# Loading the first third of the weights from SyncE's queue at the start of a fused FFT and ReGLU kernel

## The chip, the cores and the metric

The kernel runs on one core of a Trainium2 chip. The metric is the device time of one execution in microseconds (us). A ratio is the mean time of one kernel's fast runs over the mean of the other's from the same rounds, with a 95% interval, so it is not quite the ratio of the medians that are quoted beside it.

## The reference

```
x: 8 x 3008 x 256;  w_gate, w_val: 256 x 1536;  w_out: 1536 x 256   (float32)
X = real(fft(fft(x, axis=1), axis=2))            # Fourier mixing over sequence and model axis
x = X.reshape(24064, 256)
out = (maximum(x @ w_gate, 0) * (x @ w_val)) @ w_out
```

## The kernel before

The transform over the sequence is split as 94 x 32 ("stage 1" and "stage 2"); the transform over the model axis is folded into the weights: W's upper and lower 128 rows are added and subtracted, and a cosine or sine matrix (cd) is multiplied onto them ("fold"). The weights are prepared in thirds of 512 columns. The first batch has no predecessor to hide behind: its x comes in six pieces ("lo" for rows 0 to 15, "hi" for rows 16 to 31), cast from float32 to bf16 by the DMA.

```python
def load_w(n, q, which=(0, 1)):                 # one third of W_gate and W_val: four pieces of 256 KB
    for i in which:
        w = (w_gate, w_val)[i]
        for c in range(2):
            q.dma_start(out=wst[i, n, c], in_=w[c*128:(c+1)*128, n*512:(n+1)*512])
def pair_w(n, i, eng, parts=(0, 1)):            # sum into a third tile, difference in place
    lo, hi, up = (wst[i, n, c] for c in range(3))
    if 0 in parts: eng.tensor_tensor(up, lo, hi, op=ALU.add)
    if 1 in parts: eng.tensor_tensor(lo, lo, hi, op=ALU.subtract)
def fold_w(n, i, cs, ps=None):                  # TensorE, then ScalarE writes wc or ws
    for k, w in ((0, wst[i, n, 2]), (1, wst[i, n, 0])):
        nc.tensor.matmul(ps[64*k:64*k+64, :], lhsT=cd[:, cs, 64*k:64*k+64], rhs=w, start=True, stop=True)
    nc.scalar.copy((wc, ws)[cs][i][:, n*512:(n+1)*512], ps[:])
# ... cut ...
warm(WARM)                                      # 12 dummy matmuls at the start
iota(pl, si...); iota(pl, ki...)                # GpSimd (pl), in order
load_first(0, 8); ...; load_first(24, 8)        # x pieces, on GpSimd's queue
load_first(8, 4); load_first(20, 4); ...; load_first(12, 4); load_first(16, 4)
# ... cut ...
load_w(0, pl)                                   # W's first third, behind x on the same queue
# ... stage 1 tables; ends() and back() make reversed copies of each x piece on VectorE and ScalarE ...
group((1, 2, 3), False); warm(9)                # stage 1: lo products of banks 1 to 3, dummies
# ... VectorE: da, dq (for cd), bit tables ... then the hi pieces
group((1, 2, 3), True)
group((4, 5), False); warm(4); group((4, 5), True); group((6, 7, 0), False)
pair_w(0, 0, dve); group((6, 7, 0), True)       # W_gate's sum and difference on VectorE
# ... cut ...
pair_w(0, 1, pl)                                # W_val's on GpSimd
fold_w(0, 0, 0, g_tile()); upright(...); upright(...)
fold_w(0, 0, 1, psw); rotate(...); scale_w(0, 0, psw); stage2(...)
fold_w(0, 1, 0, g_tile()); stage2(...); fold_w(0, 1, 1)
# ... then 288 steps of G (gate), V (value), h and out ...
```

Of the kernel before, what the change touches and what calls it, by code (L numbers as in the profile page):

```python
# [11 lines left out]
F32 = mybir.dt.float32  # L12
BF16 = mybir.dt.bfloat16
I32 = mybir.dt.int32
ALU = mybir.AluOpType
# [13 lines left out]
def free(ap, offset, *dims):  # L29

    part = list(ap.ap[0])
    return bass.AP(ap.tensor, ap.offset + offset, [part] + [list(d) for d in dims])
# [12 lines left out]
def kernel(ctx: ExitStack, tc, x, w_gate, w_val, w_out, out):  # L45
# [3 lines left out]
    nc = tc.nc  # L49
# [14 lines left out]
    psg = ctx.enter_context(tc.tile_pool(name="psg", bufs=2, space=PS))  # L64
# [90 lines left out]
    t1t = {}  # L155
# [27 lines left out]
    psf = {}  # L183
# [41 lines left out]
    def first_evac(c, evac):  # L225

        if 0 not in t1t:
            t1t[0] = tp.tile([128, 16, D], BF16, tag="t1", bufs=1, name="t1")
        dst = free(t1t[0][:], 2 * c, [1536, 2], [16, 96], [1, 2])
        src = free(psf[c], 0, [96, 2], [1, 96], [192, 2])  # L230
        plain = nc.scalar.copy if evac == "act" else nc.vector.tensor_copy
        plain(dst, src)
        if c == 0:
            plain(free(t1t[0][0:1], 1536, [16, 96]), psf[0][0:1, 384:480])

    def upright(blk, cs, evac):

        if 0 not in t4t:
            t4t[0] = tp.tile([128, NKA, D], BF16, tag="t4", name="t4")
        ps = spare("pst") if blk else early("pst")  # L240
        for g in range(4):
            nc.tensor.matmul(ps[:, g * H:(g + 1) * H], lhsT=free(t1t[0][:], 1536 * cs + 128 * (4 * blk + g), [1, 128]),  # L242
                             rhs=perm[:], start=True, stop=True)
        dst, src = t4t[0][:, 4 * blk:4 * blk + 4, cs * H:(cs + 1) * H], ps.rearrange("p (g d) -> p g d", g=4)
        if evac == "act":
            nc.scalar.copy(dst, src)
        else:
            nc.vector.tensor_copy(dst, src)
# [17 lines left out]
    def stage2(b, blk, cs, evac):  # L266
        if (b, blk) not in pqt:
            pqt[b, blk] = pqp.tile([128, 2, 512], BF16, tag="pq", name="pq")
            nbt[b, blk] = pqp.tile([128, 512], BF16, tag="nb", name="nb")
        t4, pq = t4t[b], pqt[b, blk]  # L270
        ps = borrow("ps2") if b else early("ps2") if blk == 0 else spare("ps2")
        for g in range(4):
            nc.tensor.matmul(ps[:, g * 128:(g + 1) * 128], lhsT=t4[:, 4 * blk + g, cs * H:(cs + 1) * H],  # L273
                             rhs=m2[:, cs, :], start=True, stop=True)
        if blk == NBLK - 1:
            nc.tensor.matmul(ps[:, 496:497], lhsT=t4[:, 0, cs * H:(cs + 1) * H], rhs=m2[:, cs, 0:1], start=True, stop=True)
        if evac == "act":
            nc.scalar.copy(pq[:, cs, :], ps[:])
        else:
            nc.vector.tensor_copy(pq[:, cs, :], ps[:])  # L280
        if cs == 1 and (b or blk):

            row = view(Nd, (b * NBLK + blk) * 512, [[512, 1], [1, 512]])
            nc.sync.dma_start(out=row, in_=pq[0:1, 1, :])
            nc.sync.dma_start(out=nbt[b, blk][:], in_=view(row, 0, [[0, 128], [1, 512]]))
# [5 lines left out]
    m2 = const.tile([128, 2, 128], BF16, tag="m2")  # L291
    rot = const.tile([128, 128], BF16, tag="rot")
    perm = const.tile([128, 128], BF16, tag="perm")
    s2 = const.tile([128, 1], F32, tag="s2")
    wc = [const.tile([128, DF], BF16, tag=f"wc{i}", name=f"wc{i}") for i in range(2)]
    ws = [const.tile([128, DF], BF16, tag=f"ws{i}", name=f"ws{i}") for i in range(2)]
    wm = [const.tile([128, DF], BF16, tag=f"wm{i}", name=f"wm{i}") for i in range(2)]
# [7 lines left out]
    wst = {}  # L305
# [4 lines left out]
                wst[i, n, c] = pair[:, i, :]  # L310
    cd = hp.tile([128, 2, 512], F32, tag="h", name="cd")[:, :, 0:H]

    def load_w(n, q, which=(0, 1)):
        for i in which:
            w = (w_gate, w_val)[i]
            for c in range(2):
                q.dma_start(out=wst[i, n, c], in_=w[c * 128:(c + 1) * 128, n * 512:(n + 1) * 512])

    def pair_w(n, i, eng, parts=(0, 1)):

        lo, hi, up = (wst[i, n, c] for c in range(3))
        if 0 in parts:
            eng.tensor_tensor(up, lo, hi, op=ALU.add)
        if 1 in parts:
            eng.tensor_tensor(lo, lo, hi, op=ALU.subtract)

    def scale_w(n, i, ps):

        nc.vector.tensor_scalar(wm[i][:, n * 512:(n + 1) * 512], ps[:], scalar1=s2[:], scalar2=None, op0=ALU.mult)

    def fold_w(n, i, cs, ps=None):

        ps = ps or spare("psw")
        for k, w in ((0, wst[i, n, 2]), (1, wst[i, n, 0])):
            nc.tensor.matmul(ps[64 * k:64 * k + 64, :], lhsT=cd[:, cs, 64 * k:64 * k + 64], rhs=w,  # L335
                             start=True, stop=True)
        sl_ = slice(n * 512, (n + 1) * 512)
        nc.scalar.copy((wc, ws)[cs][i][:, sl_], ps[:])
        if cs and (n or i):
            scale_w(n, i, ps)  # L340
# [8 lines left out]

    with tc.tile_pool(name="sp", bufs=1, space=SB) as sp:  # L350
        dve, pl = nc.vector, nc.gpsimd

        def residue(t, q, n, eng):

# [14 lines left out]
        def iota(eng, out, pattern, base, mult):  # L369
            eng.iota(out, pattern=pattern, base=base, channel_multiplier=mult, allow_small_or_imprecise_dtypes=True)  # L370
# [8 lines left out]
        mi = sp.tile([128, 1], F32, tag="mi")  # L379
        dd = sp.tile([128, H], F32, tag="dd")  # L380
# [4 lines left out]
        ui = sp.tile([128, 4, NB], F32, tag="ui")  # L385
        di = sp.tile([128, 4, 2, 16], F32, tag="di")
# [9 lines left out]
        def warm(n):  # L396

            for k in range(n):
                nc.tensor.matmul(psk[:], lhsT=wk[:, 512:640], rhs=wk[:, 0:512], start=True, stop=True)
# [14 lines left out]
        iota(pl, free(dd[:], 0, [64, 2], [1, 64]), [[1, 2], [2, 64]], 0, 0)  # L414
        load_first(12, 4)
        load_first(16, 4)
        pl.tensor_scalar(perm[:], dd[:], scalar1=mi[:], scalar2=None, op0=ALU.is_equal)
        iota(pl, ui[:], [[1, 4], [0, NB]], 0, 0)
        iota(pl, kbi[:, 0, :], [[1, NB]], NB // 2, 0)
        iota(pl, kbi[:, 1:4, :], [[0, 3], [1, NB]], 0, 0)  # L420
        load_w(0, pl)

        def angles(lo, hi):
            t, q = tt[:, lo:hi, :], tq[:, lo:hi, :]
# [10 lines left out]
        def bits(shift, mask):  # L435
            ti = sp.tile([128, 1], I32, tag=f"b{shift}{mask}i")
            dve.tensor_scalar(ti[:], pi[:], scalar1=shift, scalar2=mask,
                              op0=ALU.logical_shift_right, op1=ALU.bitwise_and)
            tf = sp.tile([128, 1], F32, tag=f"b{shift}{mask}f")
            dve.tensor_copy(tf[:], ti[:])  # L440
            return tf
# [29 lines left out]
        absolute(dq[:], da[:])  # L471
        cosines(cd[:, 0, 1:H], dq[:, 1:H], D)
        sines(cd[:, 1, 1:H], da[:, 1:H], D, 1.0)
        jj, sl, up, odd = bits(0, 15), bits(4, 1), bits(5, 3), bits(0, 1)

        ends(24, 8)
        back(25, 3, "act")
# [15 lines left out]
        sv, ti = [], []  # L493
# [3 lines left out]
            sv.append(sp.tile([128, 4, NB], F32, tag=f"m2s{cs}", name="sv"))  # L497
            pl.tensor_scalar(ti[cs], kbi[:], scalar1=mul[:], scalar2=(o0, o1)[cs][:], op0=ALU.mult, op1=ALU.add)
        dve.tensor_scalar(tabs["wzn"][:], wz[:, 0], scalar1=-1.0, scalar2=None, op0=ALU.mult)
        dve.tensor_copy(cd[:, 1, 0:1], odd[:])  # L500
        dve.tensor_scalar(cd[:, 0, 0:1], odd[:], scalar1=-1.0, scalar2=1.0, op0=ALU.mult, op1=ALU.add)
        dve.tensor_scalar(ui[:], ui[:], scalar1=up[:], scalar2=-1.0, op0=ALU.is_equal, op1=ALU.mult)

        group((4, 5), False)
        warm(4)
        ends(20, 4)
        back(20, 4, "dve")
        group((4, 5), True)
# [9 lines left out]
        load_w(2, nc.sync)  # L518
        load_x(1, 0, nc.sync, False)
        first_evac(5, "act")  # L520
        pair_w(0, 0, dve)
        for cs in range(2):
            nc.scalar.activation(sv[cs][:], ti[cs], ACTF.Sin, scale=2.0 * math.pi / NB * (1.0 - 2e-7), bias=npi[:])
        group((6, 7, 0), True)
# [1 line left out]
        first_evac(7, "act")  # L526
        first_evac(0, "dve")
        for cs in range(2):
            dve.tensor_tensor(m2[:, cs, :].rearrange("p (u k) -> p u k", u=4), sv[cs][:], ui[:], op=ALU.mult)

        iota(pl, di[:], [[-32, 4], [-16, 2], [-1, 16]], 0, 1)
        pl.tensor_scalar(s2[:], mi[:], scalar1=1.0, scalar2=-2.0, op0=ALU.min, op1=ALU.mult)
        ro = rot[:].rearrange("p (u s j) -> p u s j", u=4, s=2)
        pl.tensor_scalar(ro[:, :, 0, 1:16], di[:, :, 0, 1:16], scalar1=16.0, scalar2=-1.0,
                         op0=ALU.is_equal, op1=ALU.mult)
        pl.tensor_scalar(ro[:, :, 1, 1:16], di[:, :, 1, 1:16], scalar1=-16.0, scalar2=None, op0=ALU.is_equal)
        pl.tensor_scalar(ro[:, :, :, 0], di[:, :, :, 0], scalar1=0.0, scalar2=None, op0=ALU.is_equal)

        def g_tile():
            return psg.tile([128, 512], F32, tag="g", name="psw")  # L540

        pair_w(0, 1, pl)
        pl.iota(ix[:], pattern=[[-1, 2], [4 * NA, B]], base=4 * NA - 1, channel_multiplier=-4)
        pl.tensor_scalar(ix[:], ix[:], scalar1=0, scalar2=None, op0=ALU.max)
        fold_w(0, 0, 0, g_tile())
        upright(0, 0, "act")
        upright(0, 1, "dve")
        psw = g_tile()
        fold_w(0, 0, 1, psw)
        rotate(0, 0, 4, dve.tensor_copy)  # L550
        scale_w(0, 0, psw)
        stage2(0, 0, 0, "act")
        fold_w(0, 1, 0, g_tile())
        stage2(0, 0, 1, "dve")
        fold_w(0, 1, 1)

        pair_w(1, 0, pl)
# [227 lines left out]
    n = len(steps) // 2  # L785
# [86 lines left out]
```

## Time and profile before

| | before |
|---|---|
| median, lowest, highest of three executions | 625.28, 624.44, 625.51 us |
| span of the profiled execution | 623.1 us |
| TensorE busy | 612.1 us, 98% |
| first x piece landed, "hi" piece landed | 6.1 us, 9.2 us |
| first hi product of stage 1, end of stage 1, first G matmul | 9.75, 15.62, 21.63 us |

The profile is read in this order. The page gives busy shares. The chain of work that ended last goes backwards from the last instruction and gives at each step what released it, so it says what the time consists of; a piece is one line with its start and length. The timeline then says, for one engine, what stood ahead of a piece and what it waited for (in square brackets). The lines that carry this are shown in the prediction.

### The profile page before, as it was taken

What the parts mean: (1) busy time and instruction counts of PE and PEld (TensorE: products, weight loads), DVE (VectorE), ACT (ScalarE), POOL (GpSimd) and SP (SyncE); (2) the same over time, 40 slices, a digit from 0 to 9 for tenths busy, and PEclk for the clock granted to TensorE, in tenths of its full rate; (3) what the DMA queues carried; (4) which work ended last, traced back from release to release, by engine and by line L of the source; (5) the groups of instructions that cost most, each with busy time, mean ns of one, the idle gap of its engine ahead of it and who ended that gap; (6) DMA issues with size and microseconds to landing.
All of it is one profiled execution on the core that took longest, in us unless ns stands there. A gap on an engine that the chain in (4) does not pass through costs nothing.

```text
span 623.1 us, 11916 instructions
## 1 busy us (share of the span) xinstructions
PE 612.1 (98%) x4252; PEld 409.3 (66%) x4284; DVE 536.5 (86%) x652; ACT 444.4 (71%) x855; POOL 520.2 (83%) x447
## 2 busy tenths in 40 slices
PE   8999999999999999999999999999999999999996
PEld 5345666666666666666667666766666666666665
DVE  7677898899889898988988998898988889899991
ACT  7677777777777767767777777767677676766660
POOL 8998998998898898899988998888988965555664
PEclk9999999999999999999999999999999999999998
DMA  8984282425452182613843255531822134112114
GB/s 169 241 163 114 83 220 77 123 66 169 118 145 71 41 228 79 155 36 89 221 102 90 66 162 126 138 77 34 223 82 59 34 86 124 52 34 67 34 35 99
DMA packets 42037, 67.44 MB, mean 108 GB/s; under 512 B 5877, under 2 KB 31774, under 8 KB 39962
## 3 DMA queue, kind: packets, MB, share of 16 engines
q1 hardware_dynamic: 37162, 50.61, 31.2%
q0 software_dynamic: 4656, 15.88, 10.8%
q8 instruction: 33, 0.54, 0.4%
q14 instruction: 26, 0.21, 0.1%
q10 hardware_dynamic: 160, 0.20, 0.1%
HBM read 38.85 MB, written 30.17 MB: 111 GB/s over the span
## 4 chain that ended last, share of the span: by engine, by line
PE 96%; DMA 1%; issue 1%; ACT 1%; DVE 1%; POOL 0%; POOLq 0%
PE po L685 40%; PE V L635 19%; PE G L619 10%; PE G L626 10%; PE G L620 10%; PE psw L335 2%; PE ps L164 2%; PE ps L273 2%; DMA hi<-in_x_dram,ixf 1%; PE ps L218 1%; PE pst L242 0%; PE ps L168 0%; ACT gs L621 0%; ACT gm L628 0%; DVE h L656 0%
## 5 line engine op out<-in xcount | busy, mean ns | idle before, releaser
L656 POOL TENSOR_TENSOR h<-gm,E 128x992 bf16<-128x992 f32 (+1 forms) x138 | 320.0, 2319 | 82.8 <-DVE E L663 52.0
L685 PE MATMUL po<-wo,h 128*128 128x256 bf16 (+2 forms) x2304 | 328.4, 272 | 0.4
L685 PEld LDWEIGHTS <-h 128*128 128x128 bf16 (+2 forms) x2304 | 231.4, 103 | 105.9
L628 ACT ACTIVATE gm<-G 128x496 f32<-128x496 f32 (+1 forms) x288 | 170.6, 592 | 94.2 <-PE G L626 87.2
L649 DVE TENSOR_TENSOR h<-gs,V 128x1024 bf16<-128x1024 f32 (+3 forms) x150 | 173.9, 1159 | 66.0 <-PE V L635 41.2
L642 DVE SCALAR_TENSOR_TENSOR E<-nb,af,V 128x496 f32<-128x496 bf16 (+1 forms) x276 | 190.2, 730 | 0.7 <-PE V L635 0.7
L621 ACT ACTIVATE gs<-G 128x497 f32<-128x497 f32 (+2 forms) x288 | 169.6, 589 | 23.7 <-PE G L620 23.7
L663 DVE SCALAR_TENSOR_TENSOR E<-E,V 128x992 f32<-128x992 f32 (+1 forms) x138 | 164.4, 1191 | 0.0
L619 PE MATMUL G<-pq,wc 128*128 128x496 bf16 (+2 forms) x286 | 107.2, 375 | 1.1
L626 PE MATMUL G<-pq,wm 128*128 128x496 bf16 (+1 forms) x288 | 107.9, 375 | 0.3
L620 PE MATMUL G<-pq,ws 128*128 128x497 bf16 (+2 forms) x288 | 107.9, 375 | 0.1
L635 PE MATMUL V<-pq,ws 128*128 128x496 bf16 (+2 forms) x280 | 83.7, 374 | 0.0
L635 PE MATMUL V<-pq,wc 128*128 128x496 bf16 (+2 forms) x267 | 80.9, 374 | 0.8 <-DVE h L656 0.8
L620 PEld LDWEIGHTS <-ws 128*128 128x128 bf16 x288 | 28.2, 98 | 32.6
L698 ACT COPY os<-po 128x512 f32<-128x512 f32 x63 | 36.9, 586 | 14.3 <-PE po L685 12.5
L115 POOL TENSOR_TENSOR eo<-xla 94x256 bf16<-94x256 f32 x56 | 40.7, 733 | 0.6
L635 PEld LDWEIGHTS <-wc 128*128 128x128 bf16 x288 | 28.2, 98 | 19.7 <-issue 1.3
L619 PEld LDWEIGHTS <-wc 128*128 128x128 bf16 x288 | 28.2, 98 | 19.1 <-issue 1.1
L179 ACT CAST t<-ps 96x512 bf16<-96x512 f32 x56 | 32.7, 584 | 4.0 <-PE ps L164 1.9
L115 POOL TENSOR_TENSOR eo<-xlb 94x256 bf16<-94x256 f32 (+1 forms) x42 | 34.5, 823 | 0.7
L112 POOL TENSOR_TENSOR xla<-xla,xha 94x510 f32<-94x510 f32 x28 | 32.9, 1175 | 2.2
L626 PEld LDWEIGHTS <-wm 128*128 128x128 bf16 x288 | 28.1, 98 | 4.4 <-issue 1.6
(140 smaller groups left out, 366.7 us busy)
## 6 DMA issues: line engine op xcount, KB each, us to landing
out_dram<-os SPq DMA_DIRECT2D x124, 128.0 KB
Td<-t SPq DMA_DIRECT2D x7, 768.0 KB
t<-Td SPq DMA_DIRECT2D x7, 768.0 KB
out_dram<-os SPq DMA_DIRECT2D x82, 64.0 KB
xla<-in_x_dram SPq DMA_DIRECT2D x7, 720.0 KB
xlb<-in_x_dram SPq DMA_DIRECT2D x6, 640.0 KB
nb<-Nd SPq DMA_DIRECT2D x23, 128.0 KB
out_dram<-os SPq DMA_DIRECT2D x40, 48.0 KB
```

Of the source, the lines that this page charges most:

```text
L115: yield eng.tensor_tensor(e1[:, :, k:k + H], x1[:, :, 0:H], free(x1, D, [DX, n], [-1, H]), op=op)
L619: nc.tensor.matmul(G[:, ds], lhsT=wc[0][:, fs], rhs=pq[:, 0, ds], start=True, stop=False)
L620: nc.tensor.matmul(G[:, ds], lhsT=ws[0][:, fs], rhs=pq[:, 1, ds], start=False, stop=True)
L621: nc.scalar.activation(pair(t, "gs")[:, t % 2, ds], G[:, ds], ACTF.Relu)
L626: nc.tensor.matmul(G[:, cols], lhsT=wm[0][:, f * 128:(f + 1) * 128], rhs=pqt[b, blk][:, 1, cols], start=False, stop=True, skip_group_check ...
L628: nc.scalar.activation(pair(t, "gm")[:, t % 2, cols], G[:, cols], ACTF.Relu)
L635: nc.tensor.matmul(o, lhsT=w[:, f * 128:(f + 1) * 128], rhs=pqt[b, blk][:, min(k, 1), cs], start=(k == 0), stop=(k > 0 or split(t)), skip_ ...
L642: nc.vector.scalar_tensor_tensor(pair(t, "E")[:, t % 2, cols], nbt[b, blk][:, cols], af[:, f:f + 1], pair(t, "V")[:, t % 2, cols], op0=ALU ...
L649: nc.vector.tensor_tensor(pair(t, "h")[:, k, 0, 0:ds.stop - ds.start], pair(t, "gs")[:, k, ds], val, op=ALU.mult)
L656: eng.tensor_tensor(free(pair(t, "h")[:], 1024 * (t % 2) + 512 + w - 1, [1024, n], [-1, w]), pair(t, "gm")[:, k, cols], val[:, :, cols], o ...
L663: nc.vector.scalar_tensor_tensor(E[:, :, cols], E[:, :, cols], 2.0, V[:, :, cols], op0=ALU.mult, op1=ALU.subtract)
L685: nc.tensor.matmul(po[0:m, i, :], lhsT=pair(t - f + ff, "h")[:, ff % 2, sg, g * 128:g * 128 + m], rhs=wo[:, ff, :], start=(ff == 0), stop= ...
```

## The change

Its intent is to take one of the four folds of the first third out of the stretch between stage 1 and the first G, and into a gap of stage 1 that dummy matmuls filled. For that W_gate has to be there early: three of the four W pieces become SyncE's first instructions, GpSimd sums W_gate, VectorE sums W_val later.

```diff
+        load_w(0, nc.sync, ((0, 0), (0, 1), (1, 0)))        # ahead of everything
 ...
-        pl.tensor_scalar(perm[:], dd[:], ...)
+        load_w(0, pl, ((1, 1),))
+        pair_w(0, 0, pl)
 ...
-        load_w(0, pl)
 ...
         group((4, 5), False)
-        warm(4)
+        fold_w(0, 0, 0, g_tile())
         ends(20, 4)
 ...
-        pair_w(0, 0, dve)
+        pair_w(0, 1, dve)
 ...
-            dve.tensor_tensor(m2[:, cs, :]..., sv[cs][:], ui[:], op=ALU.mult)
+            pl.tensor_tensor(m2[:, cs, :]..., sv[cs][:], ui[:], op=ALU.mult)
 ...
-        pair_w(0, 1, pl)
-        fold_w(0, 0, 0, g_tile())
+        psw = g_tile()
+        turned(0, 1, psw)                                   # the matmuls of a fold, without its copy
         upright(0, 0, "act")
         upright(0, 1, "dve")
+        nc.scalar.copy(ws[0][:, 0:512], psw[:])
+        nc.scalar.mul(wm[0][:, 0:512], psw[:], s2[:])
 ... (cut: the one-row piece of bank 0 goes to ScalarE, sign tables to GpSimd, two columns of cd earlier,
     ScalarE's copy of the third fold later)
```

More of the change, by code (lines that the diff above doesn't have):

```diff
@@ L233, in first_evac @@
         if c == 0:
-            plain(free(t1t[0][0:1], 1536, [16, 96]), psf[0][0:1, 384:480])
+            nc.scalar.copy(free(t1t[0][0:1], 1536, [16, 96]), psf[0][0:1, 384:480])
     def upright(blk, cs, evac):
@@ L311, with load_w @@
     cd = hp.tile([128, 2, 512], F32, tag="h", name="cd")[:, :, 0:H]
-    def load_w(n, q, which=(0, 1)):
-        for i in which:
+    def load_w(n, q, parts=((0, 0), (0, 1), (1, 0), (1, 1))):
+        for i, c in parts:
             w = (w_gate, w_val)[i]
-            for c in range(2):
-                q.dma_start(out=wst[i, n, c], in_=w[c * 128:(c + 1) * 128, n * 512:(n + 1) * 512])
+            q.dma_start(out=wst[i, n, c], in_=w[c * 128:(c + 1) * 128, n * 512:(n + 1) * 512])
     def pair_w(n, i, eng, parts=(0, 1)):
@@ L329, in scale_w, with turned @@
         nc.vector.tensor_scalar(wm[i][:, n * 512:(n + 1) * 512], ps[:], scalar1=s2[:], scalar2=None, op0=ALU.mult)
-    def fold_w(n, i, cs, ps=None):
-        ps = ps or spare("psw")
+    def turned(n, cs, ps, i=0):
         for k, w in ((0, wst[i, n, 2]), (1, wst[i, n, 0])):
@@ L336, in fold_w @@
                              start=True, stop=True)
+    def fold_w(n, i, cs, ps=None):
+        ps = ps or spare("psw")
+        turned(n, cs, ps, i)
         sl_ = slice(n * 512, (n + 1) * 512)
@@ L416 @@
         load_first(16, 4)
-        pl.tensor_scalar(perm[:], dd[:], scalar1=mi[:], scalar2=None, op0=ALU.is_equal)
+        load_w(0, pl, ((1, 1),))
+        pair_w(0, 0, pl)
         iota(pl, ui[:], [[1, 4], [0, NB]], 0, 0)
@@ L473 @@
         sines(cd[:, 1, 1:H], da[:, 1:H], D, 1.0)
-        jj, sl, up, odd = bits(0, 15), bits(4, 1), bits(5, 3), bits(0, 1)
+        odd, jj, sl, up = bits(0, 1), bits(0, 15), bits(4, 1), bits(5, 3)
+        dve.tensor_copy(cd[:, 1, 0:1], odd[:])
+        dve.tensor_scalar(cd[:, 0, 0:1], odd[:], scalar1=-1.0, scalar2=1.0, op0=ALU.mult, op1=ALU.add)
         ends(24, 8)
@@ L499, with g_tile @@
         dve.tensor_scalar(tabs["wzn"][:], wz[:, 0], scalar1=-1.0, scalar2=None, op0=ALU.mult)
-        dve.tensor_copy(cd[:, 1, 0:1], odd[:])
-        dve.tensor_scalar(cd[:, 0, 0:1], odd[:], scalar1=-1.0, scalar2=1.0, op0=ALU.mult, op1=ALU.add)
-        dve.tensor_scalar(ui[:], ui[:], scalar1=up[:], scalar2=-1.0, op0=ALU.is_equal, op1=ALU.mult)
+        pl.tensor_scalar(ui[:], ui[:], scalar1=up[:], scalar2=-1.0, op0=ALU.is_equal, op1=ALU.mult)
+        pl.tensor_scalar(perm[:], dd[:], scalar1=mi[:], scalar2=None, op0=ALU.is_equal)
+        iota(pl, di[:], [[-32, 4], [-16, 2], [-1, 16]], 0, 1)
+        pl.tensor_scalar(s2[:], mi[:], scalar1=1.0, scalar2=-2.0, op0=ALU.min, op1=ALU.mult)
+        def g_tile():
+            return psg.tile([128, 512], F32, tag="g", name="psw")
         group((4, 5), False)
-        warm(4)
+        fold_w(0, 0, 0, g_tile())
         ends(20, 4)
@@ L528 @@
         for cs in range(2):
-            dve.tensor_tensor(m2[:, cs, :].rearrange("p (u k) -> p u k", u=4), sv[cs][:], ui[:], op=ALU.mult)
-        iota(pl, di[:], [[-32, 4], [-16, 2], [-1, 16]], 0, 1)
-        pl.tensor_scalar(s2[:], mi[:], scalar1=1.0, scalar2=-2.0, op0=ALU.min, op1=ALU.mult)
+            pl.tensor_tensor(m2[:, cs, :].rearrange("p (u k) -> p u k", u=4), sv[cs][:], ui[:], op=ALU.mult)
         ro = rot[:].rearrange("p (u s j) -> p u s j", u=4, s=2)
@@ L537 @@
         pl.tensor_scalar(ro[:, :, :, 0], di[:, :, :, 0], scalar1=0.0, scalar2=None, op0=ALU.is_equal)
-        def g_tile():
-            return psg.tile([128, 512], F32, tag="g", name="psw")
-        pair_w(0, 1, pl)
         pl.iota(ix[:], pattern=[[-1, 2], [4 * NA, B]], base=4 * NA - 1, channel_multiplier=-4)
         pl.tensor_scalar(ix[:], ix[:], scalar1=0, scalar2=None, op0=ALU.max)
-        fold_w(0, 0, 0, g_tile())
+        psw = g_tile()
+        turned(0, 1, psw)
         upright(0, 0, "act")
         upright(0, 1, "dve")
+        nc.scalar.copy(ws[0][:, 0:512], psw[:])
+        nc.scalar.mul(wm[0][:, 0:512], psw[:], s2[:])
         psw = g_tile()
-        fold_w(0, 0, 1, psw)
+        turned(0, 0, psw, 1)
         rotate(0, 0, 4, dve.tensor_copy)
-        scale_w(0, 0, psw)
         stage2(0, 0, 0, "act")
-        fold_w(0, 1, 0, g_tile())
         stage2(0, 0, 1, "dve")
+        nc.scalar.copy(wc[1][:, 0:512], psw[:])
         fold_w(0, 1, 1)
```

## The prediction

> **What bounds the kernel now.** I read the page first, then the chain of work that ended last, cut to the first 24 us, then the timelines of VectorE, ScalarE, GpSimd and the SyncE queue there, and last the busy time by stretches. The page says where the time is:
>
> ```profile
> PE 612.1 (98%) x4252; PEld 409.3 (66%) x4284; DVE 536.5 (86%) x652; ACT 444.4 (71%) x855; POOL 520.2 (83%) x447
> ...
> PE 96%; DMA 1%; issue 1%; ACT 1%; DVE 1%; POOL 0%; POOLq 0%
> ```
>
> TensorE is the bound for practically the whole 623.1 us. The change touches only what comes before the first product of the feed-forward part (G, written from wc and pq). After that point no DMA and no GpSimd piece of any length stands in the chain, only TensorE with a few ScalarE and VectorE pieces around 37 and 44 to 51 us. So I assume that whatever the start gains or loses is passed on whole, and the question is only when the first G matmul begins. In the chain of before that is 21.63 us:
>
> ```profile
> 3.04 6.14 DMA hi<-in_x_dram,ixf
> ...
> 9.75 1.82 PE ps L218 x20
> 11.57 0.06 issue
> 11.63 0.81 PE psk L399 x3
> 12.44 0.63 PE ps L218 x6
> ...
> 15.62 1.74 PE psw L335 x4
> 17.36 0.55 PE pst L242 x8
> 17.91 1.01 PE psw L335 x4
> 18.92 0.11 PE psr L261
> 19.04 0.24 PE ps L273 x4
> 19.28 1.01 PE psw L335 x4
> 20.29 0.33 PE ps L273 x4
> 20.62 1.01 PE psw L335 x4
> 21.63 0.32 PE G L619
> ```
>
> Columns: start, length, engine, tile written, line. The reader is to see three stretches. To 9.7 us TensorE waits for the second x piece (the "hi" load of eight rows). From 9.75 to 15.6 it does stage 1 (ps), with dummy matmuls (psk, which only keep it busy) in a gap before 12.44. From 15.62 to 21.63 come the four folds of the first third of the weights (psw), each 1.01 us of TensorE, the first stretched to 1.74 by waiting 0.73 us, and between them the transposes (pst), the rotation (psr) and two stage-2 products. VectorE's timeline names the waits of that stretch:
>
> ```profile
> 14.82 0.69 DVE L323 TENSOR_TENSOR wst<-wst 128x512 f32<-128x512 f32 x1 [0.43 <-DMA wst<-in_moe_w_gate_dram]
> 15.54 0.69 DVE L325 TENSOR_TENSOR wst<-wst 128x512 f32<-128x512 f32 x1
> 16.15 0.55 DVE L232 CAST t<-ps 128x384 bf16<-128x384 f32 x1
> 16.74 0.56 DVE L234 CAST t<-ps 1x96 bf16<-1x96 f32 x1
> ```
>
> W_gate arrives at 14.8, its sum and difference end at 16.23 (the first fold's second half starts at 16.29), then the last stage-1 bank is cast, with its one-row piece, until 17.30, and the transposes start at 17.3.
>
> **What the Trainium skill says.** (1) "DMA: Bandwidth & Descriptors", section "Issuing engines are not separate DMA queues": transfers of all issuers run on the same 16 engines and interleave. The trace agrees that the engines, not the issuers, are full while x arrives, and that the W loads behind x go at nearly twice the rate:
>
> ```profile
> 2.00:4.00 2.00, 2.00 (x6) 0.75 (x5) 1.90 (x5) 0.86 (x4) 1.60 (x5) 1.00 0.61 68
> ...
> 6.00:12.00 6.00, 5.30 (x43) 3.71 (x45) 4.87 (x32) 5.60 (x15) 5.61 (x14) 1.00 1.05 186
> 12.00:14.50 2.50, 2.40 (x27) 1.88 (x25) 1.79 (x8) 1.59 (x4) 2.33 (x6) 1.00 1.02 363
> ```
>
> (each row: stretch, length, busy times of PE, PEld, DVE, ACT, POOL, granted clock, DMA share, GB/s; the share 1.05 means all engines taken, while 2 to 4 us leaves 0.39 of them free). (2) The same page, "SWDGE vs HWDGE vs iDMA": a cast during a DMA needs GpSimd, a plain copy can go from SyncE. x is cast to bf16, W is not, so only W can move to SyncE. (3) "GPSIMD Engine Reference", section 4.1: a two-input elementwise operation is some 2 times slower there than on VectorE. The trace agrees: the same 128x512 addition takes 0.69 us on VectorE and 1.27 on GpSimd. (4) The same page, "Key points": GpSimd and VectorE share SBUF interfaces; the trace shows only a spread of 1.26 to 1.40 us in these additions.
>
> **The change part by part.**
> Loads: three of four W pieces (256 KB each) leave GpSimd's queue, where they were last, and are SyncE's first instructions. They can be issued from about 0.8 us; in this trace a load's first bytes flow 1.1 to 1.6 us after its issue starts, so from about 2 us. Three pieces are 0.79 MB, at 363 GB/s 2.2 us of all DMA engines. Free before 6 us are about 0.8 us (2 us x 0.39) and a gap of 0.2 between 5.5 and 6 us, perhaps more since the first x packets are slow in any case. So 0.8 to 1.2 us of W fall on the x loads, which arrive one behind the other (9.2, 10.1, about 11.4, 12.4, 13.5 us) at the engines' rate. I choose 0.8 us of delay.
> Sums of W_gate: on GpSimd, 2 x 1.27 us plus gaps, from about 9.1 us (after its last issue) to 11.8, no longer waiting for anything.
> First fold within stage 1: it replaces four dummy matmuls (about 0.85 us) by 1.01 us. With x 0.8 later TensorE starts the hi products at 10.55; 12 of them take 1.0 and 8 lo ones 0.66, so it comes to the fold at 12.2, after GpSimd is done. Then fold to 13.2, 8 hi products to 13.9, 14 lo to 15.0, 14 hi to 16.15. Stage 1 ends 0.55 us later than the 15.6 of before, of which the fold is less than 0.2.
> After stage 1: the second fold's matmuls now wait for nothing (16.15 to 17.15; 0.73 us of wait gone). The transposes wait for the last cast. VectorE sums W_val ahead of it; the fourth piece is still on GpSimd's queue behind x, so it lands at about 13.5 + 0.7 + 0.8 = 15.0. The two operations take 1.4 us, to about 16.7 with the small one before them; cast to 17.25; the one-row piece, now on ScalarE but ordered behind the cast, to about 17.6 (an estimate of 0.3). So the transposes start at 17.6 against 17.36. Behind them: transposes 0.55, third fold 1.01, rotation 0.11, stage-2 products 0.24 and 0.33, fourth fold 1.01, together 3.25, against 4.27 of before, because one fold fewer stands there. First G at about 20.9: 0.7 us earlier.
> ScalarE takes the wm scaling of W_gate from VectorE: casts of 0.59 each from 18.2 (transposes, ws, wm, pq) end near 20.6, the last two weights near 21.8, against 22.27; not the end of anything later than before.
> GpSimd gets the sign tables, about 1.2 us more, but loses a wait of 1.35, so the second third's sums start no later than the 19.32 of before.
> Sum: 625.28 - 0.7 = 624.6.
>
> **The rivals.**
> (a) The W loads ride nearly free in the idle first 4 us: x is not later, stage 1 ends at 15.4, the transposes start at 16.5 to 17.1: first G near 20.2, 624 or a little less. For it: 0.39 of the engines free from 2 to 4 us, nothing before. Against it: 2.2 us of engine time don't fit in there.
> (b) x is pushed by 1.2 us or more and W_val's last piece with it: stage 1 ends at 16.55, W_val is summed by 17.1, the cast and its row end at 18.0, first G at 21.3 or later: 625 to 626. For it: the share of 1.05 throughout.
> (c) VectorE or ScalarE becomes the bound of the start, W_val's sum holding the last cast. It is half in my sum already; it would cost up to 0.5 more.
> (d) The gain is taken back at 37 to 51 us, where ScalarE and VectorE stand in the chain. No reader of a DMA waits there, so I don't expect it.
>
> **Range and chances.** The three times of before spread over 1.1 us, as much as the effect. With (a) and (b) as the ends and that scatter, 8 in 10 lie in 623.3 to 626.0. Two per cent are 12.5 us, over half of the whole start; neither side of it can be reached by this edit: 0.005 faster, 0.99 same, 0.005 slower.
>
> **What would show it.** In the chain after: the hi load ending at 9.8 to 10.4 instead of 9.18 (the delay of x); a psw piece in place of psk near 12.2; the psw piece after stage 1 at 1.01 instead of 1.74; three folds instead of four between the end of stage 1 and the first G; G at 20.9. Wrong would be: hi at 9.2 (then a), a wait of psw for GpSimd's sums inside stage 1, or a G at 20.9 with an unchanged total, which would mean that the shift is not passed on.

## The result, and the profile after

The changed kernel takes **628.9 us** (median of six runs, 628.35 to 629.62) against 625.03 us of the kernel before (median of six, 624.44 to 625.51); the ratio is 1.0063, interval 1.005 to 1.0076. That is within 2%, but 3.9 us slower, outside the range of the prediction. The span of the profiled execution grows from 623.1 to 626.7 us. (That execution is one of the faster of the six; two took 629.62 us, and why is not shown.)

The chain of work that ended last, changed kernel, first 26 us (start, length, what):

```profile
1.41 8.36 DMA lo<-in_x_dram
...
9.81 2.10 PE ps L218 x12
11.91 2.52 PE psk L403 x9
14.44 1.76 PE ps L218 x20
16.20 1.06 PE psw L333 x4
17.28 0.59 ACT wc L341
...
20.82 1.01 PE psw L333 x4
21.82 0.63 PE pst L242 x8
22.45 1.01 PE psw L333 x4
...
24.24 1.01 PE psw L333 x4
25.25 0.32 PE G L625
```

The chain now begins with the **first** x piece (lo), which lands at 9.77 us; in the kernel before it landed 4.7 us after its issue and was not in the chain at all. Three folds stand between the end of stage 1 (20.82) and G (25.25), as intended, and the first of them is 1.01 us long, without a wait. G starts at 25.25 instead of 21.63 us: 3.62 us later, and the span is 3.6 us longer. What the start loses is passed on whole.

The timeline of the changed kernel, VectorE and GpSimd where the first x piece arrives (start, length, engine, line, what, idle time before it):

```profile
8.98 1.31 POOL L322 TENSOR_TENSOR wst<-wst 128x512 f32<-128x512 f32 x1
9.79 0.56 DVE L189 COPY back<-lo 94x8 bf16<-94x8 bf16 x1 [3.64 <-DMA lo<-in_x_dram]
...
10.25 1.55 DVE L201 COPY back<-lo 94x762 bf16<-94x762 bf16 x2
10.37 1.35 POOL L324 TENSOR_TENSOR wst<-wst 128x512 f32<-128x512 f32 x1
...
13.93 0.17 DVE L191 COPY back<-hi 94x8 bf16<-94x8 bf16 x1
```

The same VectorE operations in the timeline of the kernel before:

```profile
6.12 0.18 DVE L189 COPY back<-lo 94x8 bf16<-94x8 bf16 x1 [0.17 <-DMA lo<-in_x_dram]
...
6.21 0.58 DVE L201 COPY back<-lo 94x762 bf16<-94x762 bf16 x2
...
9.20 0.20 DVE L191 COPY back<-hi 94x8 bf16<-94x8 bf16 x1 [0.33 <-DMA hi<-in_x_dram,ixf]
```

Two things are to be seen. VectorE sits idle for 3.64 us until lo is there, and everything behind it in its queue, down to the hi copies, comes later. And the copies of lo take 2.01 us (9.79 to 11.80) where they took 0.67 (6.12 to 6.79): they run while GpSimd does W_gate's sum and difference, and the last ends within 0.1 us of GpSimd's second operation (11.72), as the first (10.35) does of GpSimd's first (10.29).

Busy times by stretch, changed kernel (stretch, length, PE, PEld, DVE, ACT, POOL, granted clock, DMA share, GB/s):

```profile
6.00:12.00 6.00, 2.63 (x15) 1.89 (x14) 2.36 (x5) 2.28 (x6) 5.61 (x10) 0.80 0.98 182
12.00:14.50 2.50, 2.50 (x11) 0.92 (x10) 2.23 (x18) 1.54 (x6) 0.23 (x2) 0.81 0.91 213
```

TensorE's granted clock was 1.00 in both stretches before and is 0.80 and 0.81 now; TensorE was idle for 3.4 us before lo came, and the nine dummies (psk) of the chain take 2.52 us.

So there are four suspects: (A) the early W loads delay x; (B) GpSimd's sums hold VectorE; (M2) the clock falls while TensorE waits; (C) ScalarE's copy of the first fold (wc at 17.28 in the chain) stands ahead of work that stage 1 needs. The rival (R) is that the new order of sums and folds itself costs. A1, A2, A3 and A-bytes below are versions of A: they differ in how the W loads delay x.

### The profile page after: what moved, and what is told of

Read it like the earlier page. It is cut to its first block, busy times and chain, and to the rows that moved or that the text cites. A ratio compares the mean times of both kernels' runs of the same rounds, so it can differ in the third digit from the quotient of the medians.

```text
span 626.7 us, 11939 instructions
## 1 busy us (share of the span) xinstructions
PE 614.3 (98%) x4280; PEld 409.8 (65%) x4280; DVE 535.2 (85%) x647; ACT 445.3 (71%) x857; POOL 520.8 (83%) x447
## 4 chain that ended last, share of the span: by engine, by line
PE 96%; DMA 1%; ACT 1%; DVE 0%; issue 0%; POOL 0%; POOLq 0%
PE po L691 40%; PE V L641 20%; PE G L632 10%; PE G L625 10%; PE G L626 10%; PE psw L333 2%; PE ps L164 2%; PE ps L273 2%; DMA lo<-in_x_dram 1%; PE ps L218 1%; PE psk L403 0%; PE pst L242 0%; PE ps L168 0%; ACT gs L627 0%; ACT gm L634 0%
## 5 line engine op out<-in xcount | busy, mean ns | idle before, releaser
L627 ACT ACTIVATE gs<-G 128x497 f32<-128x497 f32 (+2 forms) x288 | 169.6, 589 | 23.8 <-PE G L626 23.7
L625 PE MATMUL G<-pq,wc 128*128 128x497 bf16 (+2 forms) x288 | 107.9, 375 | 0.0
L641 PE MATMUL V<-pq,wc 128*128 128x497 bf16 (+2 forms) x288 | 85.4, 375 | 0.8 <-DVE h L662 0.8
L641 PE MATMUL V<-pq,ws 128*128 128x497 bf16 (+2 forms) x288 | 85.4, 374 | 0.0
```

Of the source, the lines that this page charges most:

```text
L625: nc.tensor.matmul(G[:, ds], lhsT=wc[0][:, fs], rhs=pq[:, 0, ds], start=True, stop=False)
L627: nc.scalar.activation(pair(t, "gs")[:, t % 2, ds], G[:, ds], ACTF.Relu)
L641: nc.tensor.matmul(o, lhsT=w[:, f * 128:(f + 1) * 128], rhs=pqt[b, blk][:, min(k, 1), cs], start=(k == 0), stop=(k > 0 or split(t)), skip_ ...
```

## The experiments

"First hi product" is the start of stage 1's first product of a hi piece in the timeline, "G" that of the first G matmul (the timeline's starts lie 0.07 us ahead of the chain's). Spans of profiled executions follow G in every run of the table but one (e7, by half a microsecond).

| run | median us | ratio (95%) | lo landed | first hi product | G | span |
|---|---|---|---|---|---|---|
| before | 625.0 to 625.3 | | 6.10 | 9.75 | 21.56 | 623.1 |
| changed | 628.9 | 1.0063 (1.005 to 1.0076) | 9.77 | 14.38 | 25.2 | 626.7 |
| e1_loads3 | 629.67 | 1.0062 (1.0045 to 1.0079) | 9.69 | 15.47 | 26.73 | 628.0 |
| e2_after2 | 629.55 | 1.0062 (1.0042 to 1.0082) | 7.78 | 14.08 | 27.44 | 628.9 |
| e3_after2_wclate | 627.86 | 1.0042 (1.0025 to 1.0059) | 9.13 | 14.91 | 25.35 | 626.8 |
| e4_after3_gated | 631.8 | 1.0102 (1.0085 to 1.0119) | 6.13 | 10.15 | 28.95 | 630.4 |
| e5_loads3_warm | 627.39 | 1.0034 (1.0016 to 1.0052) | 10.01 | 13.01 | 24.1 | 625.4 |
| e6_after_warm | 628.66 | 1.0056 (1.0038 to 1.0074) | 9.22 | 14.38 | 25.19 | 626.7 |
| e7_after_nosum_warm | 626.89 | 1.0025 (1.0007 to 1.0042) | 9.72 | 12.95 | 23.8 | 625.8 |
| e8_load1 | 625.79 | 1.0016 (0.9987 to 1.0046) | 6.68 | 10.92 | 22.09 | 623.6 |
| e9_w2first_pool | 628.42 | 1.0057 (1.0041 to 1.0072) | 7.80 | 12.47 | 23.5 | 625.0 |
| e10_w3first_pool_warm | 627.97 | 1.0044 (1.0028 to 1.0061) | 9.43 | 13.08 | 24.13 | 625.6 |
| n1_order | 625.15 | 1.0002 (0.9988 to 1.0015) | 6.0 | 9.66 | 21.86 | 623.2 |
| n2_xfirst | 625.1 | 1.0002 (0.9989 to 1.0016) | 5.8 | 9.75 | 21.64 | 623.1 |
| n3_order_xfirst | 625.2 | 1.0004 (0.999 to 1.0018) | 5.8 | 9.75 | 21.56 | 623.0 |

One execution of the kernel before in the rounds of e5 to e8 took 2297.69 us; it is far from all others and not used.

### e1_loads3: the loads alone

```diff
+        load_w(0, nc.sync, ((0, 0), (0, 1), (1, 0)))     # the kernel before, ahead of everything
-        load_w(0, pl)
+        load_w(0, pl, ((1, 1),))
```

> The kernel before with the loads of the change alone: three W pieces from SyncE as its first instructions, the fourth on GpSimd's queue; sums, folds and all else as before. Theory A (the early W pieces delay the x pieces): the first x piece (lo, 6.1 us before, 9.8 after) lands at 9.5 to 9.9 here too, stage 1's hi products start near 13.0 instead of 9.75, the first G near 24.5 instead of 21.63, about 628 us. Theory B (GpSimd's sum of W_gate, which shares the SBUF interfaces, slows VectorE's reversed copies of the first x piece, 0.58 to 1.55 us): those copies take 0.6 us here, because no sum runs beside them, and the hi products start about 1.4 us sooner than the 14.38 of the changed kernel. Rival R (the new arrangement of sums and folds is what costs): x lands as before, time 625.

Measured: 629.67 us, as slow as the whole change. lo lands at 9.69 us. VectorE's copies of lo take 0.19 and 0.58 us, as fast as before, since no sum runs beside them, and VectorE has the hi piece ready at 12.7 us. But the hi products start only at 15.47: the nine dummies ahead of them took 3.84 us. So A holds, R falls (nothing of the new order is in this kernel), B's term is seen, and the clock, which I had not put into this expectation, costs 2.5 us here.

### e2_after2 and e3_after2_wclate: two early pieces, and ScalarE's copy moved

```diff
-        load_w(0, nc.sync, ((0, 0), (0, 1), (1, 0)))     # e2: the changed kernel
+        load_w(0, nc.sync, ((0, 0), (0, 1)))
-        load_w(0, pl, ((1, 1),))
+        load_w(0, pl, ((1, 0), (1, 1)))
-        fold_w(0, 0, 0, g_tile())                        # e3: this in addition
+        psw = g_tile()
+        turned(0, 0, psw)
         first_evac(5, "act")
+        nc.scalar.copy(wc[0][:, 0:512], psw[:])
```

> The changed kernel with two early W pieces (W_gate) instead of three; both W_val pieces go on GpSimd's queue behind x. The two W_gate pieces had landed at 3.4 and 4.1 us in the changed kernel, before most of x moved; it is the third piece that trickled beside x until 9.9 us. Theory A1 (the overlap of the third piece with x makes some DMA engines fall behind): lo lands at 6.1 to 6.8 us, hi at 9.2 to 10.0, hi products start at 9.8 to 10.5, first G at 20.3 to 21.0, 623.5 to 624.5 us. Rival A2 (any early W traffic costs, in proportion to bytes): lo lands near 8.5, first G near 23.5, 627.

> e2_after2 with ScalarE's copy of the first fold (wc of W_gate) put behind the casts of stage 1's banks 4 and 5, where in the changed kernel it stood ahead of a reversed copy and those casts (17.28 us, then TensorE waited for ScalarE until 18.84). Theory C (that place costs stage 1 some 0.5 us): first G 0.3 to 0.5 us sooner than e2_after2 and no wait of ps for ScalarE in stage 1 beyond that of before. Rival: ScalarE's order costs nothing once x is on time; same as e2_after2 within 0.2 us.

Measured: both missed by far. The two pieces had landed by 4.1 us, yet lo came at 7.78 us in e2 and at 9.13 in e3, whose loads are the same. A1 (only the third piece's overlap hurts) falls. A2 (lo near 8.5) is neither met nor excluded: the same loads gave values 1.35 us apart, and there is one profile of each. In e2 VectorE was also held by GpSimd's two sums: two 128x128 operations, 0.23 us each elsewhere, took 1.18 and 1.30 us, while GpSimd's operations ran 1.32 and 1.26 us beside them. Its copies of lo took 1.68 us, but they ended at 9.57, and the first sum began at 9.53: GpSimd was issuing loads until then. In e1 such an issue beside the same copies did not slow them (0.58 us), so this one stays unexplained. The granted clock was 0.50 from 14.5 to 20 us, the 20 products of stage 1 took 3.38 us instead of 1.82. (The profiled execution is the slowest of e2's four; two took 628.18 and 628.57.) For C the time from the first hi product to the second fold is the measure: 6.0 us in e3 (14.91 to 20.91), 6.37 in the changed kernel (14.38 to 20.75), 6.37 and 6.36 in e6 and e7. The place of ScalarE's copy costs some 0.4 us.

### e4_after3_gated: the three pieces held back until lo has landed

```diff
         load_first(0, 8)
+        nc.sync.dma_start(out=seen[:], in_=xt[0]["lo"][0:1, 0, 0:2])     # waits for lo
+        load_w(0, nc.sync, ((0, 0), (0, 1), (1, 0)))                     # no longer ahead of everything
```

> The changed kernel with SyncE's three W pieces held back until the first x piece has landed (a tiny transfer that reads it goes ahead of them). Theory A: lo lands at 6.1 us as before; the W pieces now run beside the later x pieces, so hi lands up to 1 us late (9.2 to 10.2) and the last x piece up to 2 us late (13.5 to 15.6); first G at 21.5 to 22.5, 625 to 626 us. If also here some DMA engines fall behind by 2 us, hi lands near 11.5 and the time is near 627. If the place of the W loads didn't matter (rival R): 628.9 as changed.

Measured: lo on time at 6.13, as A has it, but 631.8 us, a miss of my numbers. hi came when A expects it too: VectorE's first copy of it, which waits for the transfer, starts at 9.69, and the first hi product at 10.15. So the first two x pieces were hardly delayed; the last came at 14.96 instead of 13.47, within A's 2 us. W was delayed: a W_gate piece needed 8.15 us from its issue and landed at 15.9 us. GpSimd's sum and the fold, which stands in the middle of stage 1, waited for it, TensorE went idle for 5.39 us, and the fold took 3.31 us: at a granted clock of 0.50 (a fold took 1.96 us at that in e2), and with a wait for GpSimd's difference in it. A fold inside stage 1 makes stage 1 wait for W.

### e5_loads3_warm, e6_after_warm, e7_after_nosum_warm: clock and sums apart

```diff
-WARM = 12
+WARM = 28                                                # e5 on e1, e6 on the changed kernel, e7 as well
-        pair_w(0, 0, pl)                                 # e7 only; wrong result on purpose
-        for k, w in ((0, wst[i, n, 2]), (1, wst[i, n, 0])):
+        for k, w in ((0, wst[i, n, 2 if n or i else 1]), (1, wst[i, n, 0])):
```

> e1_loads3 with 28 instead of 12 dummy matmuls at the very start, so that TensorE is busy until about 9.1 us. Theory M2 (the late x piece leaves TensorE idle for over 3 us, its granted clock falls to half, and the nine dummies and the products behind them take about twice as long: 3.84 us instead of 2.11 for the dummies): the clock stays at 1.00 from 6 to 14.5 us, the nine dummies take some 2.1 us, the hi products start at 12.6 to 13.2 instead of 15.5, the first G near 24.2 instead of 26.8, about 627.5 against 629.7 us. Rival: the clock has no part, TensorE waits for x and VectorE alone; no change.

> The changed kernel with 28 dummies at the start. If theories M2 and B both hold, TensorE is now ready early, but VectorE, slowed by GpSimd's sum, releases the hi products only near 14.4 as before: hi products at 14.0 to 14.4, a gain of at most 0.3 us on the changed kernel. If the clock alone explained the late hi products: they start at 13.0, a gain of 1.4 us.

> The changed kernel with 28 dummies and without GpSimd's sum and difference of W_gate's first third: the folds read the unsummed pieces, so the result is wrong on purpose. Theory B: VectorE's reversed copies of the first x piece take 0.6 us instead of 1.55, and with the clock kept up as well the hi products start at 12.6 to 13.2 instead of 14.4, first G near 23.8, 1.2 to 1.6 us under e6_after_warm. Rival: GpSimd's sum doesn't matter; same as e6_after_warm.

Measured: all three as M2 and B together say (e7's time is 1.8 us under e6's, a little more than expected). The chain of e1 and that of e5, from the dummies to the hi products:

```profile
11.83 3.84 PE psk L399 x9
15.67 1.83 PE ps L218 x20
```

```profile
11.22 1.94 PE psk L399 x9
13.17 1.67 PE ps L218 x20
```

With the clock kept at 1.00 the same nine dummies take 1.94 us, and the first hi product comes 2.46 us sooner although lo lands 0.3 us later. In the changed kernel the same measure gains nothing (e6: 14.38 and 14.38), because there VectorE was not ready sooner: held by the sums, it finished the copies of lo at 11.80 in both, though lo came 0.5 us sooner in e6. Without the sums (e7) VectorE's timeline reads

```profile
9.74 0.19 DVE L189 COPY back<-lo 94x8 bf16<-94x8 bf16 x1 [3.35 <-DMA lo<-in_x_dram]
9.83 0.48 DVE L201 COPY back<-lo 94x762 bf16<-94x762 bf16 x2
```

and the first hi product starts at 12.95, 1.43 us sooner than in e6. The result of e7 is wrong, as intended; the work is otherwise the same. That fits the Trainium skill, "SBUF — State Buffer", section "Who interferes with whom", which says that a VectorE copy in a two-port mode and a GpSimd operation take a shared pair of SBUF ports as an exclusive lock for a whole instruction; in which mode these copies ran, no run here shows. The fall of the clock fits "TensorE: Matmul & The Clock Gate", section "What's actually happening", only in part. The page has the clock at half after an idle window of some 3.4 us. In the changed kernel TensorE was idle for 3.37 us, and 0.50 was granted from 9.6 to 12.9 us. But 0.50 also followed an idle time of 1.99 us in e9 (8.4 to 11.7 us) and of 2.02 us in e2 (14.1 to 20.9 us), so here less was enough.

### e8_load1, e9_w2first_pool, e10_w3first_pool_warm: bytes or queues

```diff
+        load_w(0, nc.sync, ((0, 0),))                    # e8: the kernel before, one early piece
+        load_w(0, pl, ((0, 0), (0, 1)))                  # e9: before load_first(0, 8), GpSimd's queue
+        load_w(0, pl, ((0, 0), (0, 1), (1, 0)))          # e10: the same with three, and WARM = 28
         (the remaining pieces stay where load_w(0, pl) was)
```

> The kernel before with only one W piece (256 KB) early on SyncE, the other three on GpSimd's queue where they were. It should be in by 3.5 us, when x has hardly begun to move. If the delay of x comes from W and x sharing the DMA engines at the same time (theory A1): lo lands at 6.1 to 6.4 us, time as before, 625.3, perhaps 0.2 less because one W piece fewer lies behind x. If any use of the other queue at the start makes single DMA engines fall behind (theory A3): lo lands at 7 to 9 us with a median over the engines near 6, and the time is 626 to 629.

> The kernel before with the two W_gate pieces first of all on GpSimd's own queue, ahead of the first x piece, and no transfer on SyncE's queue. The same bytes lie ahead of x as in e2_after2 and e3_after2_wclate, but in one queue and one behind the other. If the bytes ahead are what delays x (theory A-bytes): lo lands at 7.6 to 8.4 us (1.2 us of issue and 1.4 us of transfer, partly in idle time), all 16 engines within 0.8 us of each other, and time about 626.5. If the two queues side by side make single engines fall behind (theory A3): here the spread over the engines stays near the 0.6 us of before, against 1.9 to 3.3 us in e2 and e3.

> e5_loads3_warm with its three early W pieces on GpSimd's own queue, first of all, instead of SyncE's: the same bytes ahead of x, the same 28 dummies, the same work elsewhere. GpSimd issues its first x load some 1.8 us later for it (three issues of 0.6 us). Theory A3 (two queues side by side make single DMA engines fall behind): lo lands at 8.2 to 8.8 us, sooner than the 10.0 of e5 in spite of the later issue, the 16 engines within 1 us of each other (3.9 in e5), first G at 22.8 to 23.4 against 24.14. Theory A-bytes (the delay is the bytes ahead and no more): lo lands 1.8 us later than in e5, near 11.8.

The trace records, for each load, when each of the 16 DMA engines finished its share; a load has landed with the last. For lo, in us:

```
                    W pieces, queue     lo issued   first  median  last   last - first
before              none ahead             1.41      5.49   5.72   6.10      0.6
e8_load1            1, SyncE               1.41      6.00   6.22   6.68      0.7
e2_after2           2, SyncE               1.41      5.90   6.91   7.78      1.9
e3_after2_wclate    2, SyncE               1.41      5.83   6.05   9.13      3.3
e9_w2first_pool     2, GpSimd              2.87      7.05   7.27   7.80      0.7
changed             3, SyncE               1.41      5.79   6.72   9.76      4.0
e1_loads3           3, SyncE               1.41      6.33   7.41   9.69      3.4
e5_loads3_warm      3, SyncE               1.40      6.15   7.47  10.01      3.9
e10_w3first_pool..  3, GpSimd              3.42      7.69   8.63   9.43      1.7
```

In the changed kernel 13 engines had finished lo by 7.7 us and three needed until 9.6 to 9.8; in each later x piece three are again some 1.25 us behind the other 13 (the records do not say whether the same three). With one piece A3 fails as it was put for e8 (any use of the other queue; lo at 7 to 9 us): the engines stay within 0.7 us. With two pieces A3 is borne out, as far as one profile of each run goes: on one queue the engines stay together (0.7 us), on two they don't (1.9 and 3.3). With three pieces it is half a hit. On one queue lo takes 6.0 us from issue to landing against 8.6 on two (7.8 in e6, the least of the five runs with these loads). So it lands at about the same time in spite of an issue 2.0 us later (9.43, against 10.01 in e5 and 9.22 in e6), and A-bytes (11.8) is refuted; but 9.43 is later than A3's 8.2 to 8.8, and the spread of 1.7 is more than it allowed. The first G is the same in e5 and e10 (24.1), as in e10 the 28 dummies end after lo. e9's time missed too: the clock fell again (0.72 from 6 to 12 us), and its profiled execution was the fastest of four (626.84; the others 628.35 to 628.85). e8 is inconclusive in time (one of four runs at 628.06); in its profile lo is 0.6 and hi 1.2 us late. In all these runs lo landed later than in the kernel before (6.68 to 10.01 against 6.10 us; in e9 and e10 most of it is the later issue): W pieces ahead of x cost x time on either queue, and did not ride for free in the idle DMA time of the first 3 us.

### n1_order, n2_xfirst, n3_order_xfirst: a version without early W

```diff
-        pair_w(0, 1, pl); fold_w(0, 0, 0, g_tile()); upright x2; fold_w(0, 0, 1, psw); ...   # n1, n3
+        m2 on pl; pair_w(0, 1, pl, (0,)); pair_w(0, 1, dve, (1,))
+        fold_w(0, 0, 0, g_tile()); turned(0, 1, psw); upright x2; (then as in the changed kernel)
+        load_first(0, 8)                                 # n2, n3: ahead of the iotas of si and ki
         iota(pl, si[:], ...); iota(pl, ki[:], ...)
-        load_first(0, 8)
```

> The kernel before with its loads, and of the change only the order behind stage 1: the second fold's matmuls ahead of the transposes, the one-row piece on ScalarE, the wm scaling on ScalarE, the m2 tables on GpSimd; W_val's sum on GpSimd and its difference on VectorE. Theory: TensorE's two waits there (0.2 and 0.5 us) are filled by the second fold; first G at 21.1 to 21.3 instead of 21.63, 624.9 us. Rival: the fourth W piece lands at 16.0, W_val's difference is late on VectorE and the third fold waits for it; G at 21.6, 625.2.

> The kernel before with the first x load issued ahead of GpSimd's two small iotas (0.56 us). If the arrival of x sets the whole start, every x piece lands 0.4 to 0.56 us sooner, hi at 8.7 us, first G at 21.1 to 21.25, 624.8 us; the tables of stage 1 come 0.65 us later, which the dummies hide. Rival: the tables then hold the first products and with them VectorE; no gain.

> n1_order and n2_xfirst together. If both work as their theories say they add up: first G at 20.6 to 20.9, 624.3 to 624.5 us, below the kernel before by 0.1 per cent, which 5 rounds may just tell. If the order's gain only fills the time in which W is awaited, it is there with an earlier x as well.

Measured: none gains (ratios 1.0002, 1.0002, 1.0004, all intervals around 1). In n1 the time is the rival's, but the wait is another: the difference of W_gate (not of W_val) was done at 16.6 us, and two folds in a row took 2.79 us with their waits, so that G came at 21.86. In n2 lo lands 0.3 us sooner, but the tables, issued later, hold VectorE; the first hi product is at 9.75 as before, and W_gate's sum starts at 14.75 against 14.82. I found no version that beats the kernel before.

## Why the prediction was wrong

The loss of 3.62 us up to G splits into three terms, from the timelines and chains: the first hi product comes 4.63 us later (9.75 to 14.38), stage 1 takes 0.57 us longer (5.87 to 6.44), and the stretch behind it is 1.58 us shorter (6.01 to 4.43).

- **"I choose 0.8 us of delay"** for the x loads is the step that failed. lo came 3.66 us later, hi 2.6 us. The working (bytes at 363 GB/s less the free share of the engines) took the 16 engines as one pipe; a load lands with its slowest engine, and three engines were 3 us behind the median. The trace of before could not show this: until 13.6 us only GpSimd's queue was in use there. e1 shows that the loads alone give this delay.
- The working followed **hi** ("With x 0.8 later TensorE starts the hi products at 10.55"), because hi was in the chain of before. With lo late, lo took its place: VectorE worked through its queue in program order, and from lo's arrival to the first hi product it takes 3.2 us of work in e7. hi had landed at 11.8 and waited. e7, with clock and sums out of the way, puts the x term at 3.20 us (12.95 against 9.75).
- **"Sums of W_gate: on GpSimd, 2 x 1.27 us plus gaps"** had the duration right (1.31 and 1.35) and counted no cost for VectorE; the prediction's point (4) on the Trainium skill read the sharing of SBUF interfaces as "only a spread". Its cost is 1.43 us (e6 against e7; the changed kernel, with lo at 9.77 as against 9.72 in e7, has the same 14.38 as e6). 3.20 and 1.43 are the 4.63 us.
- The prediction did not think of the **clock**. In the changed kernel it was hidden: the slowed dummies ended (14.44) when VectorE was ready too, and e6 gains nothing. Where the sums were absent it cost 2.46 us (e1 against e5).
- **"of which the fold is less than 0.2"**: stage 1 took 6.44 us (5.60 in the working, 10.55 to 16.15) and grew by 0.57, some 0.4 of it from ScalarE's copy of that fold, which stood ahead of stage 1's own copies (e3). "not the end of anything later than before" was said of ScalarE behind stage 1 only.
- **After stage 1** the mechanism was right: three folds, none waiting, 4.43 us where the sum had 4.75 (16.15 to 20.9). The transposes did not wait: with x so late, W_val was summed in time. Of the 1.58 us gained, 0.66 is the wait for W_gate (e1, with early W and the old order, takes 5.35 instead of 6.01) and 0.92 the fold moved.
- **"Passed on whole"** was right: 3.62 us at G, 3.6 in the span.
- Rival (b) had the direction, at 1.2 us, and the range ended at 626.0. Rival (c) had named VectorE and ScalarE as bounds of the start: both held it, but ahead of and within stage 1, not through W_val's sum, which ended at 18.61 us, before the last cast could start (20.85). Rival (d) had no part. The second third's sums on GpSimd, which were to "start no later than the 19.32 of before", started at 23.13, as SyncE's loads for them began 5.2 us later; the chain does not show it.

What stays open is why from one (e3) to eight (e2) of the DMA engines fall behind with two or three W pieces on SyncE's queue, whether it is the two queues side by side or SyncE's queue as such, and why x itself goes slower then than its bytes explain (e10 as well). No experiment here takes that apart further.

## What to carry to other kernels

Before moving a load ahead of another, ask which engine queues stand in order behind the displaced load, not only which wait ends last now: the chain of before named hi, and the damage came through lo. Count a displaced load by its slowest DMA engine, and expect a bulk load to cost the one behind it more than bytes over rate. Work given to an idle GpSimd was not free here where VectorE copied in the same microseconds, and a TensorE that waited for some 2 us or more paid again in its clock (e9, e2).

## What the Trainium skill lacked or had wrong

- "DMA: Bandwidth & Descriptors", "Issuing engines are not separate DMA queues", says that the queues interleave on the same engines and that other issuers save only issue time. The page does say that the engines of one transfer finish independently, but not how far apart, nor that this differs with the queue: lo took 4.7 us from issue to landing with nothing ahead, 6.0 with three W pieces ahead on its own queue, 7.8 to 8.6 with the same pieces on SyncE's queue, with 0.6, 1.7 and 2.6 to 4.0 us between first and last engine.
- No page that I read says that a plain load beside a casting load may take 8.15 us for 256 KB (e4), where the same piece took 4.5 us behind x on one queue.
- "GPSIMD Engine Reference", "Key points", names contention with VectorE without a size; here a VectorE copy of 8 elements per partition took 0.56 to 1.11 us instead of 0.18 and ended with the GpSimd operation. "SBUF — State Buffer" has the lock.
- "TensorE: Matmul & The Clock Gate", "What's actually happening", gives the half clock after an idle window of some 3.4 us. Here 0.50 followed idle times of 1.99 us (e9) and 2.02 us (e2), while idle times of 1.21 and 0.95 us shortly after each other (e2, 6 to 12 us) left it at 1.00.
